# AV of two heads in two 64-column halves of the array, with the sums of weights in a matmul group of their own

## The chip, the cores and the metric

The kernel runs on one core of a Trainium2 chip. The metric is the device time of one execution in microseconds, as the median of several runs. A core has five engines with queues of their own: PE (matmuls; PEld are its weight loads), ACT (functions by table), DVE (elementwise work), POOL (elementwise work and the issue of some DMAs) and SP (issue of DMAs). PE reads two operands from SBUF: the weights, up to 128 columns that are loaded into the array, and the moving operand, whose columns stream through. It writes its result to PSUM, in banks of 128 partitions by 512 float32.

## The reference

Four batches, eight heads, a sequence of 768, 64 elements a head. Attention with a window of 96 positions, eight global keys and a bias by distance, then a gated FFN on the heads put side by side:

```python
scores = scale * q @ k.T + bias          # per head; bias falls with distance
scores = where(is_global | is_local, scores, -1e9)
a = softmax(scores)                      # exp, divided by the sum over keys
x = (a @ v), heads side by side          # 3072 tokens x 512
out = (relu(x @ w_gate) * (x @ w_val)) @ w_out   # 512 -> 1536 -> 512
```

## The kernel before

The work is cut into eight half-batches `s` of 384 queries. Each has an attention part, `attention_pieces(s)`, and an FFN part, `ffn_pieces(c)`, for the same tokens. The FFN of half-batch `c` is woven with the attention of `c + 1` by `weave`: after each FFN item, pieces of the attention are written out in proportion. No scheduler reorders it; each engine takes its instructions in the order of the code.

Heads are handled in four pairs `p`. Keys stand on partitions in tiles `j` of 120 local keys and the 8 global ones; there are 7 tiles for a batch, of which a first half-batch uses 4 and a second half-batch 5. For a pair, `piece_qk` (line 292) makes the scores of both heads in a qk_ps bank, transposed (keys on partitions, queries along the columns), ACT takes Exp into a tile `es` (line 306) and DVE multiplies by the factors of bias and mask `m_all` (line 315). For tile `j` a head has 3 x `w` query columns, 216 at most: 216, 216, 144 and 24 in a first half-batch, 72, 168, 192, 48 and 216 in a second one.

`piece_av(s, p, e)` (line 319) is called once for each head `e` of a pair. Its matmuls (line 331) have 128 columns of weights: 64 columns of V and 64 ones, so that a bank av_ps gets the head's output on 64 partitions and the sum of its weights, repeated, on the other 64. V lies in `vbuf` with a block of 64 ones between heads and at both ends; for head 0 of a pair the slice is [V | ones], for head 1 [ones | V], so the outputs of the pair fall on partitions 0 to 63 and 64 to 127. ACT takes Ln of the sums of each head (line 340, 64 partitions each, into one tile `lnd`), after head 1 Exp of minus that for both heads (line 345, the tile `rcp`), and then DVE multiplies each head's half bank by its part of `rcp` into `xT`, the FFN's moving operand (line 348). There are two av_ps banks; the next pair's first matmul needs a bank whose readers are through.

The FFN has 24 items of four matmuls (gate, line 375, and val, line 385) and 6 items of six matmuls (output, line 394). The gate of half-batch `c` needs all four pairs of `xT`.

Half-batches 0 and 1 are special. Their queries and keys are cast and transposed on PE (`piece_t`, line 250), with copies on DVE and ACT from one tp bank; later ones are transposed by DMA. The attention of half-batch 0 has no FFN beside it. The attention of half-batch 1 is woven into eight items of FFN 0; its queries and keys are loaded by SP behind two small memsets on DVE (line 159), which stand in the order of DVE behind a piece of pair 3 of half-batch 0. V is loaded by POOL's DMAs with a cast; the eight global rows are loaded into tile 0 and spread to the other tiles by a DMA of SP (line 125). The ones are filled by `fill` (line 150): four tiles of the first buffer by DVE at the start, ahead of and between the instructions that make `dd`, from which ACT makes `m_all`; three tiles and the seven of the second buffer by POOL.

Of the kernel before, what the change touches and what calls it, by code (L numbers as in the profile page):

```python
# [8 lines left out]
FP32 = mybir.dt.float32  # L9
BF16 = mybir.dt.bfloat16  # L10
AF = mybir.ActivationFunctionType
ALU = mybir.AluOpType
# [3 lines left out]
def kernel(  # L16
# [12 lines left out]
    nc = tc.nc  # L29

    B, H, S, D = q.shape
    NG = int(n_global)
    NL = int(n_local)
    DM = H * D
# [4 lines left out]
    QH = S // 2  # L39
    NN = 3  # L40
# [4 lines left out]
    NT = -(-S // KT)  # L45
    scale = 1.0 / math.sqrt(D)
# [7 lines left out]
    for half in range(2):  # L54
        for j in range(NT):
            w0 = PK * j - 128 * half
            a, b_ = max(0, w0), min(128, w0 + WQ)
# [6 lines left out]
    const = ctx.enter_context(tc.tile_pool(name="const", bufs=1))  # L64
# [4 lines left out]
    rc_pool = ctx.enter_context(tc.tile_pool(name="rc", bufs=2))  # L69
# [15 lines left out]
    vbuf = [const.tile([128, NT, (2 * H + 1) * D], BF16, name=f"vbuf{i}") for i in range(2)]  # L85
# [29 lines left out]
    def v_dst(b, r0, r1, j):  # L115
        t = vbuf[b % 2][r0:r1, j, D:]
        return t.rearrange("p (h z) -> p h z", z=2 * D)[:, :, 0:D]
# [5 lines left out]
    def spread_v_globals(b, j0=1, j1=NT):  # L123
        t = vbuf[b % 2]
        nc.sync.dma_start(
            out=t[0:NG, j0:j1, :],
            in_=t[0:NG, 0:1, :].to_broadcast([NG, j1 - j0, (2 * H + 1) * D]))
# [22 lines left out]
    def fill(eng, i, j):  # L150
        eng.memset(vbuf[i][:, j, :].bitcast(mybir.dt.uint32), 0x3F803F80)

# [16 lines left out]
    fill(nc.vector, 0, 0)  # L169
# [31 lines left out]
    fill(nc.vector, 0, 1)  # L201
    nc.vector.tensor_scalar(dd[0:NG, 1], ga, BIG, float(NL), op0=ALU.mult, op1=ALU.max)
    nc.vector.tensor_scalar(dd[0:NG, 0], gd, BIG, float(NL), op0=ALU.mult, op1=ALU.max)
    fill(nc.vector, 0, 2)
    fill(nc.vector, 0, 3)
# [10 lines left out]
    xT_of = {}  # L216
    es_of = {}
    av_of = {}
# [100 lines left out]
    def piece_av(s, p, e):  # L319
        b, half = divmod(s, 2)  # L320
        h = 2 * p + e
        vb = vbuf[b % 2]
        av = av_psum.tile([128, 512], FP32, name="av_ps")
        av_of[s, p, e] = av
        av3 = av[:, 0:QH].rearrange("d (n p) -> d n p", n=NN)
        todo = [t for bank in banks_of_half[half] for t in bank]
        for i, (j, a, w, m) in enumerate(todo):
            es, c = es_of[s, p, j]
            c += e * NN * w
            z0 = 2 * D * h + (D if e == 0 else 0)  # L330
            nc.tensor.matmul(av3[:, :, a : a + w],  # L331
                             lhsT=vb[:, j, z0 : z0 + 128],
                             rhs=es[:, c : c + NN * w].rearrange("k (n p) -> k n p", n=NN),
                             start=(i == 0), stop=(i == len(todo) - 1),
                             skip_group_check=True)
        o0, d0 = (0, 64) if e == 0 else (64, 0)
        if e == 0:
            av_of[s, p, "l"] = rc_pool.tile([128, QH], FP32, name="lnd")
        ln = av_of[s, p, "l"]
        nc.scalar.activation(ln[o0 : o0 + 64], av[d0 : d0 + 64, 0:QH], AF.Ln, bias=0.0, scale=1.0)  # L340
        if e == 1:
            if s not in xT_of:
                xT_of[s] = xt_pool.tile([128, N_DC, QH], BF16, name="xT")
            rc = rc_pool.tile([128, QH], FP32, name="rcp")
            nc.scalar.activation(rc, ln, AF.Exp, bias=0.0, scale=-1.0)  # L345
            for e_ in range(2):
                r = slice(64 * e_, 64 * e_ + 64)
                nc.vector.tensor_tensor(xT_of[s][r, p, :], av_of[s, p, e_][r, 0:QH], rc[r],  # L348
                                        op=ALU.mult)
# [96 lines left out]
    for j in range(4, NT):  # L446
        fill(nc.gpsimd, 0, j)
# [17 lines left out]
    for j in range(NT):  # L465
        fill(nc.gpsimd, 1, j)
# [60 lines left out]
```

## Time and profile before

| | |
|---|---|
| median of 3 runs | 295.73 us (295.42 to 295.73) |
| profiled execution | 296.74 us |
| its span on the core | 295.0 us |
| PE busy | 247.5 us, 84% |
| ACT busy | 162.9 us, 55% |
| DVE busy | 142.3 us, 48% |
| POOL busy | 97.7 us, 33% |

The span is the time from the first to the last instruction on the engines; some 1.7 us of the execution lie around it. Matmuls are pipelined: a record lasts from a matmul's start to the modelled end of its results, so records overlap, and what a matmul takes from the next one is read from start to start. In the time lines below, neighbours of one kind are merged, with their count behind an x, the idle time ahead of them in brackets and what ended it.

### The profile page before, as it was taken

What the parts mean: (1) busy time and instruction counts of PE and PEld (TensorE: products, weight loads), DVE (VectorE), ACT (ScalarE), POOL (GpSimd) and SP (SyncE); (2) the same over time, 40 slices, a digit from 0 to 9 for tenths busy, and PEclk for the clock granted to TensorE, in tenths of its full rate; (3) what the DMA queues carried; (4) which work ended last, traced back from release to release, by engine and by line L of the source; (5) the groups of instructions that cost most, each with busy time, mean ns of one, the idle gap of its engine ahead of it and who ended that gap; (6) DMA issues with size and microseconds to landing.
All of it is one profiled execution on the core that took longest, in us unless ns stands there. A gap on an engine that the chain in (4) does not pass through costs nothing.

```text
span 295.0 us, 4547 instructions
## 1 busy us (share of the span) xinstructions
PE 247.5 (84%) x1536; PEld 142.5 (48%) x1536; DVE 142.3 (48%) x362; ACT 162.9 (55%) x333; POOL 97.7 (33%) x240
## 2 busy tenths in 40 slices
PE   1355887549998974799999989999999899979994
PEld 0133354324564532466456645664566456645651
DVE  7556256662435430376347625762476155623420
ACT  8456327462335852376477647764776567644321
POOL 8990139800419000770604153051514300000000
PEclk9999999766999998699999999999999999999999
DMA  7999970928950018998395639638784510001002
GB/s 180 190 204 193 226 199 1 95 15 240 248 115 37 36 67 180 266 87 161 40 144 184 107 90 181 188 60 138 122 205 81 116 73 0 2 36 71 1 8 101
DMA packets 81199, 34.57 MB, mean 117 GB/s; under 512 B 56920, under 2 KB 77912, under 8 KB 81176
## 3 DMA queue, kind: packets, MB, share of 16 engines
q1 hardware_dynamic: 49320, 26.38, 35.3%
q0 software_dynamic: 31856, 7.91, 26.9%
q8 instruction: 12, 0.20, 0.3%
q14 instruction: 11, 0.09, 0.1%
HBM read 28.38 MB, written 6.29 MB: 118 GB/s over the span
## 4 chain that ended last, share of the span: by engine, by line
PE 69%; ACT 14%; DVE 10%; issue 2%; SPq 2%; DMA 1%; POOL 0%; ACTq 0%; DVEq 0%; POOLq 0%
PE ff_ps L385 20%; PE ff_ps L375 20%; PE ff_ps L394 17%; PE av_ps L331 6%; PE qk_ps L303 6%; ACT lnd L340 4%; DVE xT L348 4%; ACT rcp L345 3%; ACT es L306 3%; DVE es L315 2%; ACT osb L399 1%; SPq L276 1%; ACT m_all L213 1%; DVE ht L387 1%; DMA kN<-kc 1%
## 5 line engine op out<-in xcount | busy, mean ns | idle before, releaser
L375 PE MATMUL ff_ps<-xT,wg 128*128 128x384 bf16 x384 | 82.8, 339 | 2.9 <-DVE xT L348 2.7
L385 PE MATMUL ff_ps<-xT,wv 128*128 128x384 bf16 x384 | 82.2, 339 | 0.2
L387 DVE TENSOR_TENSOR ht<-ff_ps,grelu 128x384 bf16<-128x384 f32 x96 | 53.2, 555 | 42.9 <-PE ff_ps L385 41.4
L378 ACT ACTIVATE grelu<-ff_ps 128x384 bf16<-128x384 f32 x96 | 46.9, 489 | 45.5 <-PE ff_ps L375 21.9
L394 PE MATMUL ff_ps<-wo_sb,ht 128*128 128x512 bf16 x288 | 67.6, 378 | 0.0
L348 DVE TENSOR_TENSOR xT<-av_ps,rcp 64x384 bf16<-64x384 f32 x64 | 35.5, 555 | 59.3 <-ACT rcp L345 57.2
L306 ACT ACTIVATE es<-qk_ps 128x432 bf16<-128x432 f32 (+2 forms) x96 | 49.3, 529 | 20.5 <-PE qk_ps L303 18.4
L315 DVE TENSOR_TENSOR es<-es,m_all 128x432 bf16<-128x432 bf16 (+6 forms) x144 | 43.1, 331 | 32.3 <-ACT es L306 31.3
L303 PE MATMUL qk_ps<-qT,kT 128*128 128x432 bf16 (+6 forms) x144 | 34.8, 309 | 21.9 <-ACT es L306 8.7
L385 PEld LDWEIGHTS <-wv 128*128 128x128 bf16 x384 | 38.1, 101 | 30.4 <-issue 9.3
L375 PEld LDWEIGHTS <-wg 128*128 128x128 bf16 x384 | 37.7, 101 | 25.5 <-issue 4.9
L340 ACT ACTIVATE lnd<-av_ps 64x384 f32<-64x384 f32 x64 | 31.0, 485 | 23.2 <-PE av_ps L331 21.8
L331 PE MATMUL av_ps<-es,vbuf 128*128 128x216 bf16 (+5 forms) x288 | 30.7, 242 | 11.3 <-DVE xT L348 11.2
L394 PEld LDWEIGHTS <-ht 128*128 128x128 bf16 x288 | 26.8, 97 | 27.2
L331 PEld LDWEIGHTS <-vbuf 128*128 128x128 bf16 x288 | 25.3, 105 | 28.0 <-issue 19.1
L270 POOL CAST qz<-qs 128x192 bf16<-128x192 f32 x48 | 16.6, 372 | 41.2 <-issue 17.5
L399 ACT COPY osb<-ff_ps 128x512 f32<-128x512 f32 x24 | 14.0, 585 | 26.2 <-PE ff_ps L394 26.2
L303 PEld LDWEIGHTS <-kT 128*128 128x128 bf16 x144 | 14.2, 102 | 28.8 <-issue 11.5
L131 POOL DMA_DIRECT2D vbuf<-in_v_dram x28 | 24.3, 876 | 0.0
L246 POOL COPY kT<-kN 128x240 bf16<-128x240 bf16 x12 | 5.0, 416 | 41.7 <-DMA kN<-kc 41.7
L345 ACT ACTIVATE rcp<-lnd 128x384 f32<-128x384 f32 x32 | 16.7, 523 | 1.0
L242 POOL COPY kT<-kN 128x360 bf16<-128x360 bf16 x12 | 6.4, 536 | 29.0 <-DMA kN<-kc 29.0
(57 smaller groups left out, 88.9 us busy)
## 6 DMA issues: line engine op xcount, KB each, us to landing
out_dram<-osb SPq DMA_DIRECT2D x24, 256.0 KB, 2.0
qs<-in_q_dram SPq DMA_DIRECT2D x6, 768.0 KB, 7.1
ks<-in_k_dram SPq DMA_DIRECT2D x6, 768.0 KB, 10.1
vbuf<-in_v_dram POOLq DMA_DIRECT2D x24, 120.0 KB, 5.0
qs<-in_q_dram SPq DMA_DIRECT2D x8, 192.0 KB, 12.5
ks<-in_k_dram SPq DMA_DIRECT2D x8, 192.0 KB, 5.1
wg<-in_moe_w_gate_dram POOLq DMA_DIRECT2D x3, 512.0 KB, 7.4
wv<-in_moe_w_val_dram POOLq DMA_DIRECT2D x3, 512.0 KB, 9.2
```

Source lines behind the costliest of these rows:

```text
L303: nc.tensor.matmul(ps[:, c : c + n_], lhsT=kt[:, j, :], rhs=qd[:, :, :, a : a + w], start=True, stop=True)
L306: nc.scalar.activation(es[:, 0:cols], ps[:, 0:cols], AF.Exp, bias=0.0, scale=scale)
L315: nc.vector.tensor_mul(e4, e4, mk)
L331: nc.tensor.matmul(av3[:, :, a : a + w], lhsT=vb[:, j, z0 : z0 + 128], rhs=es[:, c : c + NN * w].rearrange("k (n p) -> k n p", n=NN), star ...
L340: nc.scalar.activation(ln[o0 : o0 + 64], av[d0 : d0 + 64, 0:QH], AF.Ln, bias=0.0, scale=1.0)
L345: nc.scalar.activation(rc, ln, AF.Exp, bias=0.0, scale=-1.0)
L348: nc.vector.tensor_tensor(xT_of[s][r, p, :], av_of[s, p, e_][r, 0:QH], rc[r], op=ALU.mult)
L375: nc.tensor.matmul(psg[:, 0:QH], lhsT=w_of(wg, dc, fc), rhs=xT[:, dc, :], start=(dc == 0), stop=(dc == N_DC - 1))
L378: nc.scalar.activation(gr, psg[:, 0:QH], AF.Relu, bias=0.0, scale=1.0)
L385: nc.tensor.matmul(psv[:, 0:QH], lhsT=w_of(wv, dc, fc), rhs=xT[:, dc, :], start=(dc == 0), stop=(dc == N_DC - 1))
L387: nc.vector.tensor_tensor(ht[:, fc, :], psv[:, 0:QH], st["gr"], op=ALU.mult)
L394: nc.tensor.matmul(ps2, lhsT=ht[:, fc, n * 128 : (n + 1) * 128], rhs=wo_sb[:, fc, :], start=(fc == 0), stop=(fc == N_FC - 1))
```

## The change

`vbuf` now holds V alone, 512 columns a tile. A tile `ones` of 128 x 64 is set once. `piece_av(s, p, what)` is still called twice for each pair, but by kind: with `what` 0 it makes the sums of both heads, with `ones` as weights, and with `what` 1 the outputs of both heads, with V as weights. In each, every key tile has two matmuls of 64 weight columns, head 0 into partitions 0 to 63 and head 1 into partitions 64 to 127 of the same bank; the program gives them array tiles of 128 rows by 64 columns, at columns 0 and 64. After the sums ACT takes Ln and Exp on 128 partitions; after V one multiplication on 128 partitions gives `xT`. The places of the two calls in the order are those of the two heads before. The fills go; the last tile of each V buffer, whose lower part no load covers, is set to zero once.

```diff
-    vbuf = [const.tile([128, NT, (2 * H + 1) * D], BF16, name=f"vbuf{i}") for i in range(2)]
+    vbuf = [const.tile([128, NT, DM], BF16, name=f"vbuf{i}") for i in range(2)]
+    ones = const.tile([128, D], BF16)
...
     def v_dst(b, r0, r1, j):
-        t = vbuf[b % 2][r0:r1, j, D:]
-        return t.rearrange("p (h z) -> p h z", z=2 * D)[:, :, 0:D]
+        return vbuf[b % 2][r0:r1, j, :].rearrange("p (h d) -> p h d", d=D)
...
-            in_=t[0:NG, 0:1, :].to_broadcast([NG, j1 - j0, (2 * H + 1) * D]))
+            in_=t[0:NG, 0:1, :].to_broadcast([NG, j1 - j0, DM]))
...
-    def fill(eng, i, j):
-        eng.memset(vbuf[i][:, j, :].bitcast(mybir.dt.uint32), 0x3F803F80)
...
-    fill(nc.vector, 0, 0)
+    nc.vector.memset(ones, 1.0)
+    nc.vector.memset(vbuf[0][:, NT - 1, :], 0.0)
...
-    fill(nc.vector, 0, 1)
     nc.vector.tensor_scalar(dd[0:NG, 1], ga, BIG, float(NL), op0=ALU.mult, op1=ALU.max)
     nc.vector.tensor_scalar(dd[0:NG, 0], gd, BIG, float(NL), op0=ALU.mult, op1=ALU.max)
-    fill(nc.vector, 0, 2)
-    fill(nc.vector, 0, 3)
...
-    def piece_av(s, p, e):
+    def piece_av(s, p, what):
+
         b, half = divmod(s, 2)
-        h = 2 * p + e
-        vb = vbuf[b % 2]
         av = av_psum.tile([128, 512], FP32, name="av_ps")
-        av_of[s, p, e] = av
         av3 = av[:, 0:QH].rearrange("d (n p) -> d n p", n=NN)
         todo = [t for bank in banks_of_half[half] for t in bank]
         for i, (j, a, w, m) in enumerate(todo):
             es, c = es_of[s, p, j]
-            c += e * NN * w
-            z0 = 2 * D * h + (D if e == 0 else 0)
-            nc.tensor.matmul(av3[:, :, a : a + w],
-                             lhsT=vb[:, j, z0 : z0 + 128],
-                             rhs=es[:, c : c + NN * w].rearrange("k (n p) -> k n p", n=NN),
-                             start=(i == 0), stop=(i == len(todo) - 1),
-                             skip_group_check=True)
-        o0, d0 = (0, 64) if e == 0 else (64, 0)
-        if e == 0:
-            av_of[s, p, "l"] = rc_pool.tile([128, QH], FP32, name="lnd")
-        ln = av_of[s, p, "l"]
-        nc.scalar.activation(ln[o0 : o0 + 64], av[d0 : d0 + 64, 0:QH], AF.Ln, bias=0.0, scale=1.0)
-        if e == 1:
+            for e in range(2):
+                h = 2 * p + e
+                ce = c + e * NN * w
+                nc.tensor.matmul(av3[64 * e : 64 * e + 64, :, a : a + w],
+                                 lhsT=ones if what == 0 else vbuf[b % 2][:, j, D * h : D * h + D],
+                                 rhs=es[:, ce : ce + NN * w].rearrange("k (n p) -> k n p", n=NN),
+                                 start=(i == 0), stop=(i == len(todo) - 1),
+                                 skip_group_check=True)
+        if what == 0:
+            ln = rc_pool.tile([128, QH], FP32, name="lnd")
+            nc.scalar.activation(ln, av[:, 0:QH], AF.Ln, bias=0.0, scale=1.0)
+            rc = rc_pool.tile([128, QH], FP32, name="rcp")
+            nc.scalar.activation(rc, ln, AF.Exp, bias=0.0, scale=-1.0)
+            av_of[s, p] = rc
+        else:
             if s not in xT_of:
                 xT_of[s] = xt_pool.tile([128, N_DC, QH], BF16, name="xT")
-            rc = rc_pool.tile([128, QH], FP32, name="rcp")
-            nc.scalar.activation(rc, ln, AF.Exp, bias=0.0, scale=-1.0)
-            for e_ in range(2):
-                r = slice(64 * e_, 64 * e_ + 64)
-                nc.vector.tensor_tensor(xT_of[s][r, p, :], av_of[s, p, e_][r, 0:QH], rc[r],
-                                        op=ALU.mult)
+            nc.vector.tensor_tensor(xT_of[s][:, p, :], av[:, 0:QH], av_of[s, p], op=ALU.mult)
...
-    for j in range(4, NT):
-        fill(nc.gpsimd, 0, j)
...
-    for j in range(NT):
-        fill(nc.gpsimd, 1, j)
+    nc.gpsimd.memset(vbuf[1][:, NT - 1, :].bitcast(mybir.dt.uint32), 0)
```

PE's order at the seam between the two pieces of pair 0 of half-batch 0; es0 to es2 are the pair's score tiles, the number behind av_ps tells one bank's use from another's. Before, the last key tile of head 0 and then head 1:

```order
L331 LDWEIGHTS vbuf0_101
L331 MATMUL av_ps_297<-es2_223,vbuf0_101 128x3x8
L331 LDWEIGHTS vbuf0_101
L331 MATMUL av_ps_304<-es0_213,vbuf0_101 128x3x72
L331 LDWEIGHTS vbuf0_101
L331 MATMUL av_ps_304<-es1_218,vbuf0_101 128x3x72
```

And now the end of the sums and the beginning of V:

```order
L325 LDWEIGHTS ones_103
L325 MATMUL av_ps_296<-es2_222,ones_103 64x3x8
L325 LDWEIGHTS vbuf0_101
L325 MATMUL av_ps_309<-es0_212,vbuf0_101 64x3x72
L325 LDWEIGHTS vbuf0_101
L325 MATMUL av_ps_309<-es0_212,vbuf0_101 64x3x72
L325 LDWEIGHTS vbuf0_101
L325 MATMUL av_ps_309<-es1_217,vbuf0_101 64x3x72
```

Each tile of `es` now has two matmuls in a row, one for each head, on 64 partitions, and each bank holds both heads.

DVE's order in half-batch 0, from the last mask of pair 2's scores over the copies of pair 3's queries and keys (qT, kT) to the first mask of pair 3's. Before:

```order
L315 TENSOR_TENSOR es_291<-es_291,m_all 128x48
L348 TENSOR_TENSOR xT<-av_ps,rcp 64x384 x2
L262 COPY qT_111<-tp 64x384
L263 COPY qT_111<-tp 64x384
L243 COPY kT_3_106<-tp 128x24
L244 COPY kT_3_106<-kT_3_106 128x7x8
L348 TENSOR_TENSOR xT<-av_ps,rcp 64x384 x2
L315 TENSOR_TENSOR es_345<-es_345,m_all 128x432
```

And now:

```order
L310 TENSOR_TENSOR es_290<-es_290,m_all 128x48
L339 TENSOR_TENSOR xT<-av_ps,rcp 128x384
L257 COPY qT_112<-tp 64x384
L258 COPY qT_112<-tp 64x384
L238 COPY kT_3_107<-tp 128x24
L239 COPY kT_3_107<-kT_3_107 128x7x8
L339 TENSOR_TENSOR xT<-av_ps,rcp 128x384
L310 TENSOR_TENSOR es_356<-es_356,m_all 128x432
```

One multiplication into xT stands where two stood, ahead of the copies and ahead of the masks; nothing else changes place.

## Rows read from the trace of the kernel before

**Rows 1.** The page, part 1: busy us, share of the span, instructions.

```profile
PE 247.5 (84%) x1536; PEld 142.5 (48%) x1536; DVE 142.3 (48%) x362; ACT 162.9 (55%) x333; POOL 97.7 (33%) x240
```

**Rows 2.** Waits of PE: who for whom, us in total, times, longest.

```profile
PE av_ps L331 <- DVE xT L348: 11.2, 10, 1.9
...
PE ff_ps L375 <- DVE xT L348: 2.7, 2, 1.3
```

**Rows 3.** Groups by line and shape: count, busy us, mean ns, idle before.

```profile
L348 DVE TENSOR_TENSOR xT<-av_ps,rcp 64x384 bf16<-64x384 f32 x64 | 35.5, 555 | 59.3 <-ACT rcp L345 57.2 <-PE ff_ps L375 1.2
L340 ACT ACTIVATE lnd<-av_ps 64x384 f32<-64x384 f32 x64 | 31.0, 485 | 23.2 <-PE av_ps L331 21.8
...
L331 PEld LDWEIGHTS <-vbuf 128*128 128x128 bf16 x288 | 25.3, 105 | 28.0 <-issue 19.1 <-DVE xT L348 0.3
...
L345 ACT ACTIVATE rcp<-lnd 128x384 f32<-128x384 f32 x32 | 16.7, 523 | 1.0
```

**Rows 4.** Time line of PE, half-batch 4: start us, us, what, count.

```profile
155.45 0.81 PE L375 MATMUL ff_ps<-xT,wg 128*128 128x384 bf16 x4
156.10 0.42 PE L331 MATMUL av_ps<-es,vbuf 128*128 128x216 bf16 x4
156.38 0.81 PE L385 MATMUL ff_ps<-xT,wv 128*128 128x384 bf16 x4
...
175.13 0.42 PE L331 MATMUL av_ps<-es,vbuf 128*128 128x216 bf16 x4 [0.75 <-DVE xT L348]
```

**Rows 5.** Time line of PE, half-batch 7.

```profile
253.92 0.47 PE L331 MATMUL av_ps<-es,vbuf 128*128 128x72 bf16 x5
254.23 0.81 PE L385 MATMUL ff_ps<-xT,wv 128*128 128x384 bf16 x4
```

**Rows 6.** Time line of PE and DVE, half-batch 0.

```profile
19.18 1.18 PE L331 MATMUL av_ps<-es,vbuf 128*128 128x216 bf16 x8
...
20.21 0.80 PE L257 MATMUL tp<-ident,qk 128*128 128x128 bf16 x6
...
22.08 1.28 PE L331 MATMUL av_ps<-es,vbuf 128*128 128x216 bf16 x8 [1.07 <-DVE xT L348]
...
24.47 0.88 PE L303 MATMUL qk_ps<-qT,kT 128*128 128x432 bf16 x2 [1.11 <-ACT lnd L340]
...
27.32 0.06 DVE L159 MEMSET qs<- 1x4 f32 x1
...
29.12 1.28 PE L331 MATMUL av_ps<-es,vbuf 128*128 128x216 bf16 x8 [1.71 <-DVE xT L348]
...
32.70 0.48 PE L375 MATMUL ff_ps<-xT,wg 128*128 128x384 bf16 x1 [1.34 <-DVE xT L348]
```

**Rows 7.** Time line of POOL and PE, half-batch 1.

```profile
40.74 0.51 POOL L227 CAST qk<-ks 128x384 bf16<-128x384 f32 x1 [2.38 <-DMA ks<-in_k_dram]
...
42.83 0.49 PE L257 MATMUL tp<-ident,qk 128*128 128x128 bf16 x6 [1.11 <-DVE kT L248]
...
55.00 0.52 PE L303 MATMUL qk_ps<-qT,kT 128*128 128x432 bf16 x1 [3.16 <-ACT es L306]
```

**Rows 8.** Time line of DVE and ACT, the start.

```profile
1.21 0.51 DVE L151 MEMSET vbuf<- 128x544 uint32 x1
...
3.62 0.51 DVE L151 MEMSET vbuf<- 128x544 uint32 x1
...
4.53 3.73 ACT L213 ACTIVATE m_all<-dd 128x432 bf16<-128x432 f32 x8 [0.43 <-DVE dd L203]
```

**Rows 9.** One stretch: length, busy PE, PEld, DVE, ACT, POOL, PEclk, DMA, GB/s.

```profile
42.80:66.40 23.60, 14.06 (x106) 9.35 (x107) 14.59 (x46) 13.77 (x30) 14.70 (x28) 0.83 0.55 36
```

**Rows 10.** The chain in order of time, after it: start us, us, what.

```profile
66.79 1.28 PE ff_ps L385 x4
...
72.65 0.65 PE ff_ps L375 x4
```

## The prediction

> **What bounds the kernel now.** I read the busy times first, then who waits for whom on PE, then the time line of PE in the even stretch, and then of all engines in the two half-batches that stand ahead of it. PE is the busiest engine, 247.5 us of the span of 295.0, DVE and ACT are at about half [rows 1]. So an operation saved on ACT or DVE counts where PE waits for it, and a matmul column added counts nearly everywhere. The waits of PE [rows 2] say where the first can be: the AV matmuls wait for DVE's multiplication into xT ten times, 11.2 us in all, and the gate matmuls wait for the last xT of a half-batch twice, 2.7 us. The reason is in the buffers: a pair of heads takes both av_ps banks, and neither is given back before Ln, Ln, Exp and two multiplications are through. By their durations [rows 3] that is 2 x 485 + 523 + 2 x 555 = 2.6 us, less what overlaps. In the even stretch PE does two 1.3 us FFN items meanwhile and waits 0.75 us only where AV pieces of two pairs stand close together [rows 4].
>
> The even stretch, from half-batch 2 on, has PE back to back. An AV piece of a first half-batch starts at 156.10 and the next group at 156.38 [rows 4]: 0.28 us for 600 columns (216, 216, 144 and 24). A piece of a second half takes 253.92 to 254.23, 0.31 us, for 696 columns [rows 5]. Both are what the columns take one after another at the full clock, with weight loads hidden although each is recorded with 105 ns [rows 3]. That is the number on which this prediction turns.
>
> **The change, part by part. ACT and DVE.** Ln runs once a pair on 128 partitions instead of twice on 64, the multiplication into xT too. The time goes by the 384 columns, so each pair saves 485 ns on ACT and 555 ns on DVE [rows 3], 15.5 and 17.8 us over 32 pairs. On the even stretch this is hidden under PE. What counts is what the order gives: sums come first, so Ln and Exp run while V's matmuls run; the sums' bank is free after one Ln, V's after one multiplication. Then (a) the 11.2 us of AV waits go; (b) the last pair of half-batches 0 and 1 has after its last matmul one multiplication (0.56) instead of Ln, Exp and two multiplications, and the gate's first three matmuls cover that: the 2.7 us go; (c) two QK waits of 1.11 us at 24.47 [rows 6] and 3.16 us at 55.00 [rows 7] have one multiplication and one Ln less queued ahead of their copies on DVE and ACT, 1.04 us each, 2.1 us.
>
> **Start.** Two of the four fills of V's ones on DVE, 0.51 us each, stand ahead of dd, for which the masks of m_all wait [rows 8]. They become two smaller memsets. ACT itself is busy with copies to within 0.43 us of m_all's start, so (d) at most 0.4 us. The ten fills on POOL, the shorter V rows in the spread, and V's memset hide beside DMA that POOL's next casts wait for; I take nothing for them.
>
> Sum of (a) to (d): 11.2 + 2.7 + 2.1 + 0.4 = 16.4 us.
>
> **What is late next.** Half-batch 1's keys: POOL's cast at 40.74 waited for the DMA and ends at 41.25, and PE's transposes that need it started at 42.83 [rows 7]. So of what half-batch 0 gains before them, 1.07 + 1.71 + 1.34 + 1.04 + 0.4 = 5.6 us [rows 6], only 1.6 us fit if the loads land when they did. The loads are issued behind a memset on DVE at 27.32 [rows 6] that itself moves up by about 1.9 us (one Ln and one multiplication of pair 0, the start, and the Ln of pair 1 that no longer precedes the Exp of pair 3's scores). If they land that much sooner, 3.5 us fit. I take 2.6 us.
>
> The granted clock is 0.83 over half-batch 1's stretch, with PE idle for 40% of it, and after it four FFN groups take 1.28 us each where they later take 0.65 [rows 9, 10]: 2.5 us at the half level. With fewer gaps they may run at the full one, or the fall may come at another place; I take 0 and leave 2.5 us either way in the ranges.
>
> **PE.** Before, one matmul of 128 weight columns gives V and sums of one head. After, each of the two pieces of a pair has a matmul for each head, 64 columns of weights in its half of the array: twice the matmuls (576 for 288) with the same moving columns each. The trace shows no matmul in less than the whole array, so the cost is bounded. Below: the two halves stream side by side, a piece stays at 0.28 or 0.31 us, extra 0. Above: they take turns, as every two matmuls in this trace do, and a piece doubles: 24 x 0.28 + 24 x 0.31 = 14.2 us in half-batches 2 to 7. In half-batch 0 a piece takes (20.21 - 19.18) / 2 = 0.51 us [rows 6] and is on the path only where Ln or the multiplication is waited for, about four of its eight: 2.1 us; in half-batch 1 likewise half of eight at 0.4, 1.6 us. With turns half-batch 0 then gains 5.6 - 2.1 = 3.5 and gives back only 0.9. Weight loads: two of half the size where one was, hidden as the 105 ns are now; 0, with the bound in the first rival.
>
> I take the turns, since these are the only rows there are on two matmuls. Sum: -16.4 + 0.9 + 14.2 + 2.1 + 1.6 = +2.4 us. The profiled execution took 296.74 us (span 295.0 and 1.7 around it), so 299.1 there; its time is 1.0 above the median of the runs, 295.73, so **298.1 us** as a median.
>
> **Rivals. First, the halves overlap.** Then PE pays nothing and half-batch 0 gives back 5.6 - 2.6 = 3.0 us: -16.4 + 3.0 = -13.4, 282.3 us. For it: the two matmuls use other columns of the array, other moving data and other PSUM partitions. Against it: no row shows two matmuls at a time. If loads of 64 weights show, at half of 105 ns each, a pair of halves can't go faster than 0.105 us against 0.092 for 216 columns; eight loads then take 0.42 us for 0.28 and ten 0.52 for 0.31, on 48 pieces +8.4 us: 290.7. The Trainium skill, "TensorEngine Tiling (Array Packing)", Key Properties, says that tiles operate independently and can load and multiply in parallel; by that rule this rival is the case. No row here can show it.
>
> **Second, the array empties at each change between whole and half.** A change stands wherever AV work meets FFN or QK work: 100 runs' ends in the new order, 86 of them from half-batch 2 on. Price: four gate matmuls are recorded with 0.81 us and the next group starts 0.65 us after them [rows 4], so 0.16 us of a group's end lies under the next group today. If the next must wait for that, 86 x 0.16 = 13.8 us. With turns 298.1 + 13.8 = 311.9, with overlap 282.3 + 13.8 = 296.1. The same page and section says that changing the tiling mode, not just the tile, drains TensorE; by that rule this rival holds on top of either. The rows can't tell.
>
> **Third, the waits come back in another place:** V's piece of the next pair needs V's bank, which waits for Exp and its multiplication. Where two pairs stand side by side (ends of half-batches 0, 1, 2 and 7), and where ACT's queue holds other work ahead of Ln, half of the 11.2 and all of the 2.1 could stay: with turns 298.1 + 7.7 = 305.8. Against it: ACT is at 55% [rows 1], and in the even stretch an FFN item stands between.
>
> The first rival ends faster, the others and the forecast slower; what decides is the extra time of a piece on PE. Per piece 0.29 us is the turns, 0 is overlap; the two cancel the gain of 13 to 15 us where a piece costs about 0.25 us more on some 56 pieces.
>
> **How the numbers follow.** Turns 0.40, its own range 292 to 304 (gains of 16.4 less a quarter to a half, or all of the keys' slack). Overlap 0.36. Emptying 0.17, two thirds of it with turns. Waits elsewhere 0.07. About 0.2% (0.6 us) is what a measurement can tell from no change. Faster: 0.35 of the overlap and 0.09 of the turns' lower end, 0.44; same: 0.03 of the turns, 0.03 of overlap with emptying, 0.06; slower 0.50. The range runs from the overlap to emptying with turns, 282 to 312.
>
> **What would show it.** The starts of AV matmuls: in an even stretch a piece of eight takes 0.55 us with turns, 0.28 with overlap; a pair of halves starting within a few ns says overlap. The gap from the last FFN matmul's start to the first AV matmul, and back: 0.16 for FFN as now, about 0.32 if the array empties. PE's wait for xT at L331's successor: near 0 of 11.2. First gate matmul stalled on xT in half-batch 0 by less than 0.3 us; half-batch 1's transposes waiting for POOL's cast. Wrong it would be if pieces get dearer than twice, or if the gains of half-batches 0 and 1 end in the DMA wait entirely.

## The result

The changed kernel takes 285.2 us (median of 4 runs, 284.1 to 285.9) where the kernel before takes 295.6: a ratio of 0.965, 95% interval 0.961 to 0.968. Here and below, medians and ratios leave out the few runs in which a kernel was in the chip's slower state. The profiled execution has a span of 283.5 us, 11.4 less than before. The range of the prediction held it; its forecast, 298.1 and slower, had the wrong sign. The first rival, halves that overlap, was the case, with about half of the second's price on top of it.

**The profile after.** The busy line of the page, and under it the shares of the chain that ended last; compare with [rows 1]:

```profile
PE 250.5 (88%) x1824; PEld 138.6 (49%) x1824; DVE 123.0 (43%) x328; ACT 147.7 (52%) x301; POOL 93.7 (33%) x231
...
PE 77%; ACT 7%; DMA 6%; DVE 4%; SPq 3%; issue 1%; POOL 0%; ACTq 0%; DVEq 0%; POOLq 0%
```

PE has 288 more matmuls and 3 us more busy time, in a shorter span. ACT and DVE lost 15 and 19 us of busy time, for 15.5 and 17.8 worked out (DVE lost its fills too). Who waits for whom on PE, first rows of that view (us in total, times, longest), to be set against [rows 2], and the two groups that answer to [rows 3]:

```profile
PE qk_ps L298 <- DVE kT L239: 8.2, 3, 3.5
PE qk_ps L298 <- ACT es L301: 6.2, 10, 1.6
PE tp L252 <- DVE qk L222: 4.3, 1, 4.3
PE qk_ps L298 <- DMA qT<-qz: 4.1, 1, 4.1
PE av_ps L325 <- ACT lnd L332: 1.7, 4, 0.6
```

```profile
L339 DVE TENSOR_TENSOR xT<-av_ps,rcp 128x384 bf16<-128x384 f32 x32 | 17.8, 555 | 37.2 <-PE av_ps L325 29.9 <-ACT rcp L334 5.7 <-ACT grelu L368 1.1
...
L332 ACT ACTIVATE lnd<-av_ps 128x384 f32<-128x384 f32 x32 | 15.8, 494 | 17.4 <-PE av_ps L325 17.4
...
L325 PEld LDWEIGHTS <-vbuf 128*64 128x64 bf16 x288 | 11.6, 114 | 10.1 <-issue 10.1
```

Of the 11.2 us that AV waited for xT, 0.4 are left, and 1.7 us have come in which it waits for one Ln; the gate's waits for xT are gone. An operation on 128 partitions takes what one on 64 took (555 ns for 555, and 494 for 485), so half of the time is saved.

The time line of PE in half-batch 4, the place of [rows 4] (start us, us, what, count):

```profile
142.39 0.81 PE L365 MATMUL ff_ps<-xT,wg 128*128 128x384 bf16 x4
143.13 0.45 PE L325 MATMUL av_ps<-es,ones 128*64 128x216 bf16 x8
143.51 0.82 PE L375 MATMUL ff_ps<-xT,wv 128*128 128x384 bf16 x4
```

A visit to the AV matmuls takes 143.51 - 143.13 = 0.38 us for 0.28 before, and the FFN group ahead of it 143.13 - 142.39 = 0.74 for 0.65. Eight matmuls with 1200 moving columns in all fit in 0.38 us: the halves run at the same time. About 0.09 us is lost on entering and 0.08 to 0.10 on leaving. The raw starts in the trace say the same: the two halves of a pair start 3 to 4 ns apart, and the next pair 0.12, 0.09 and 0.06 us later, the distances at which single matmuls of 216, 216 and 144 columns stood before, with 0.03 more at the first.

The time line of PE over the ends of half-batches 0 and 1, the places of [rows 6 and 7]:

```profile
23.31 0.52 PE L298 MATMUL qk_ps<-qT,kT 128*128 128x432 bf16 x2 [1.01 <-ACT lnd L332]
...
26.84 0.71 PE L325 MATMUL av_ps<-es,vbuf 128*64 128x216 bf16 x8 [0.58 <-ACT lnd L332]
27.49 1.46 PE L365 MATMUL ff_ps<-xT,wg 128*128 128x384 bf16 x4
...
38.48 0.34 PE L252 MATMUL tp<-ident,qk 128*128 128x128 bf16 x3 [0.24 <-POOL qk L222]
...
49.64 0.34 PE L298 MATMUL qk_ps<-qT,kT 128*128 128x432 bf16 x1 [1.58 <-ACT es L301]
...
55.45 1.11 PE L365 MATMUL ff_ps<-xT,wg 128*128 128x384 bf16 x4
56.40 0.81 PE L375 MATMUL ff_ps<-xT,wv 128*128 128x384 bf16 x4
57.05 0.81 PE L365 MATMUL ff_ps<-xT,wg 128*128 128x384 bf16 x4
```

The four gate matmuls from 27.49 wait for nothing; before, the fourth of them waited 1.34 us [rows 6]. And after half-batch 1 the second FFN group takes 57.05 - 56.40 = 0.65 us, the full granted clock, where four groups took 1.28 [rows 10]. The stretch that answers to [rows 9], same columns:

```profile
38.20:62.20 24.00, 18.37 (x180) 11.16 (x180) 14.33 (x46) 14.10 (x31) 12.99 (x26) 1.00 0.93 142
```

PE was busy for 77% of it, not 60%, and the granted clock stayed 1.00 (the 2.4 GHz level) for 0.83.

**Where the time went**, by the start of the same matmul in both traces (after minus before): -4.3 us at the fourth gate matmul of FFN 0, -4.9 at the first transposes of half-batch 1, -8.4 at its end (the gate matmul at 55.45), -12.8 eight gate items later (66.15 us in the changed kernel), -14.1 at the first gate matmul of FFN 2 (99.32), and from there on 2.7 us are lost again: -11.4 at the end. So the gain is all made in the first 100 us, and the even stretch is a small loss. The 4.5 us that are gained between the matmuls at 55.45 and 66.15 are for the greater part the granted clock: before, it was at its half level from 61.7 to 72.0 us, in the changed kernel at the full level from 32.2 to 103.9 us.

### The profile page after: what moved, and what is told of

It reads as the page before. It is cut to its first block, busy times and chain, and to the rows that moved or that the text cites. A ratio compares the mean times of both kernels' runs of the same rounds, so it can differ in the third digit from the quotient of the medians.

```text
span 283.5 us, 5047 instructions
## 1 busy us (share of the span) xinstructions
PE 250.5 (88%) x1824; PEld 138.6 (49%) x1824; DVE 123.0 (43%) x328; ACT 147.7 (52%) x301; POOL 93.7 (33%) x231
## 4 chain that ended last, share of the span: by engine, by line
PE 77%; ACT 7%; DMA 6%; DVE 4%; SPq 3%; issue 1%; POOL 0%; ACTq 0%; DVEq 0%; POOLq 0%
PE ff_ps L375 21%; PE ff_ps L384 21%; PE ff_ps L365 21%; PE av_ps L325 8%; PE qk_ps L298 6%; DMA ks<-in_k_dram 5%; ACT es L301 2%; SPq L271 1%; ACT m_all L208 1%; DVE es L310 1%; SPq L274 1%; DMA kN<-kc 1%; SPq L111 1%; DVE qT L258 1%; ACT lnd L332 1%
## 5 line engine op out<-in xcount | busy, mean ns | idle before, releaser
L375 PE MATMUL ff_ps<-xT,wv 128*128 128x384 bf16 x384 | 80.7, 334 | 0.0
L365 PE MATMUL ff_ps<-xT,wg 128*128 128x384 bf16 x384 | 80.4, 332 | 0.1
L298 PE MATMUL qk_ps<-qT,kT 128*128 128x432 bf16 (+6 forms) x144 | 33.9, 304 | 20.7 <-DVE kT L239 8.2
L375 PEld LDWEIGHTS <-wv 128*128 128x128 bf16 x384 | 37.1, 100 | 26.6 <-issue 3.9
L365 PEld LDWEIGHTS <-wg 128*128 128x128 bf16 x384 | 36.3, 99 | 24.6 <-issue 1.8
L339 DVE TENSOR_TENSOR xT<-av_ps,rcp 128x384 bf16<-128x384 f32 x32 | 17.8, 555 | 37.2 <-PE av_ps L325 29.9
L389 ACT COPY osb<-ff_ps 128x512 f32<-128x512 f32 x24 | 14.1, 586 | 30.2 <-PE ff_ps L384 30.2
L332 ACT ACTIVATE lnd<-av_ps 128x384 f32<-128x384 f32 x32 | 15.8, 494 | 17.4 <-PE av_ps L325 17.4
L325 PEld LDWEIGHTS <-ones 128*64 128x64 bf16 x288 | 11.4, 113 | 13.4 <-issue 12.7
L325 PE MATMUL av_ps<-es,vbuf 128*64 128x216 bf16 (+6 forms) x288 | 15.7, 237 | 1.6 <-ACT lnd L332 1.2
L325 PEld LDWEIGHTS <-vbuf 128*64 128x64 bf16 x288 | 11.6, 114 | 10.1 <-issue 10.1
## 6 DMA issues: line engine op xcount, KB each, us to landing
qs<-in_q_dram SPq DMA_DIRECT2D x8, 192.0 KB, 12.8
```

Source lines behind the costliest of these rows:

```text
L298: nc.tensor.matmul(ps[:, c : c + n_], lhsT=kt[:, j, :], rhs=qd[:, :, :, a : a + w], start=True, stop=True)
L325: nc.tensor.matmul(av3[64 * e : 64 * e + 64, :, a : a + w], lhsT=ones if what == 0 else vbuf[b % 2][:, j, D * h : D * h + D], rhs=es[:, ce ...
L332: nc.scalar.activation(ln, av[:, 0:QH], AF.Ln, bias=0.0, scale=1.0)
L339: nc.vector.tensor_tensor(xT_of[s][:, p, :], av[:, 0:QH], av_of[s, p], op=ALU.mult)
L365: nc.tensor.matmul(psg[:, 0:QH], lhsT=w_of(wg, dc, fc), rhs=xT[:, dc, :], start=(dc == 0), stop=(dc == N_DC - 1))
L375: nc.tensor.matmul(psv[:, 0:QH], lhsT=w_of(wv, dc, fc), rhs=xT[:, dc, :], start=(dc == 0), stop=(dc == N_DC - 1))
```

## The experiments

The theories. **Overlap**: the two halves run at once, a change between whole and half array costs about 0.19 us a visit (a visit is one run of AV matmuls between other work), and what is gained at the front is gained by saved operations and the new order. **Turns**, the forecast: halves follow one another, and the gain comes from elsewhere. Each edit is against the changed kernel, and the diffs show its main lines. The runs were made on several chips, and the changed kernel itself was not run again beside them. The kernel before was, with medians of 295.3 to 296.0 us, so a difference from the changed kernel's 285.2 of under a microsecond says nothing.

### The order of the halves

```diff
-        for i, (j, a, w, m) in enumerate(todo):
-            es, c = es_of[s, p, j]
-            for e in range(2):
-                h = 2 * p + e
+        for e in range(2):
+            h = 2 * p + e
+            for i, (j, a, w, m) in enumerate(todo):
+                es, c = es_of[s, p, j]
```

> The changed kernel with the two loops of piece_av swapped: all key tiles of head 0 in the left half of the array, then all of head 1 in the right half, so that two matmuls in a row use the same half. Same matmuls, same columns, same order of everything else. If the halves streaming side by side carries the gain, a piece takes twice its 0.28 or 0.31 us: 48 pieces from half-batch 2 on cost 14.2 us more and the first two some 3, 285.2 + 14 to 17 = 299 to 302 us, slower than the kernel before. If the gain is the new order and the fewer operations on ACT and DVE alone, nothing changes: 285 us. If weights of 64 columns in the same half can't be loaded under the running matmul, it is dearer still, over 303.

Measured: 287.4 us, ratio to before 0.970 (0.966 to 0.975). PE's time line, half-batch 4:

```profile
143.64 0.81 PE L365 MATMUL ff_ps<-xT,wg 128*128 128x384 bf16 x4
144.38 0.46 PE L325 MATMUL av_ps<-es,ones 128*64 128x216 bf16 x8
144.77 0.82 PE L375 MATMUL ff_ps<-xT,wv 128*128 128x384 bf16 x4
```

The edit did not make turns: the visit takes 0.39 us again. By the trace's records the matmuls start in pairs of equal size (216, 216; 216, 216; 144, 144; 24, 24), 13 ns apart, although the program issues all of head 0 ahead of all of head 1; in a second half-batch, with five sizes, head 1's follow head 0's by 0.06 us. So the edit put none of the expectations to the test; it took another way to get turns, the two that follow.

### Turns on the whole array

V between blocks of zeros, ones between blocks of zeros, so that each head has a matmul of 128 weight columns that adds zeros to the other's half; order and operations of the changed kernel, but the layout and fills of before.

```diff
-                nc.tensor.matmul(av3[64 * e : 64 * e + 64, :, a : a + w],
-                                 lhsT=ones if what == 0 else vbuf[b % 2][:, j, D * h : D * h + D],
+                z0 = 2 * D * h + (D if e == 0 else 0)
+                nc.tensor.matmul(av3[:, :, a : a + w],
+                                 lhsT=ones[:, D * e : D * e + 128] if what == 0 else vbuf[b % 2][:, j, z0 : z0 + 128],
```

> The new order, one Ln and one multiplication a pair, but no halves: V lies between blocks of zeros, the ones likewise, and each head's matmul has 128 columns of weights, [V | 0] or [0 | V], that add into the same bank. Twice the matmuls of the kernel before, each on the whole array, no change between whole and half. This is the turns of the prediction: its sum says 298.1. By the changed kernel's trace: 285.2 + 14.2 + about 3 in the first half-batches - 43 visits x 0.18 us = 294 to 295. If changes between whole and half cost nothing, 302.

Measured: 293.0 us, ratio 0.989 (0.986 to 0.992). PE's time line, half-batch 4:

```profile
148.31 0.69 PE L334 MATMUL av_ps<-es,vbuf 128*128 128x216 bf16 x8
148.86 0.81 PE L374 MATMUL ff_ps<-xT,wg 128*128 128x384 bf16 x4
149.51 0.35 PE L306 MATMUL qk_ps<-qT,kT 128*128 128x432 bf16 x1
```

Here are the turns as they were priced: 0.55 us a piece (148.86 - 148.31), and no gap ahead of the next group. This is the case that the forecast of 298.1 describes, only that it still has the old layout and fills, which the forecast had gone. So at least 5 us of my error lie outside the question of turns: even with turns the kernel is faster than before.

### Turns within one half

The two calls made by head again, sums and V of head 0 in the left half of two banks, then both of head 1 in the right half. Both banks are held until the end of the pair, as before the change.

```diff
-            for e in range(2):
-                h = 2 * p + e
...
+        for what in range(2):
+            av3 = av_of[s, p][what][:, 0:QH].rearrange("d (n p) -> d n p", n=NN)
```

> Visits by head instead of by kind: one visit has the sums and the V products of head 0, all in the left half, the next those of head 1, all in the right half; Ln, Exp and one multiplication after the second. Same matmuls in halves, but a visit never has work for both halves. If each half takes its matmuls in turn and the two only run side by side when both have work, a visit takes 0.55 or 0.62 us and its two changes 0.18: 14.2 us more from half-batch 2 on, and both banks are held until the end as in the kernel before, so some waits for xT return: 299 to 306 us. If 64-column matmuls are cheap for another reason than the side by side, 286 to 290.

Measured: 303.3 us, ratio 1.026 (1.020 to 1.032): slower than before.

```profile
150.74 0.45 PE L326 MATMUL av_ps<-es,ones 128*64 128x216 bf16 x4
151.04 0.43 PE L326 MATMUL av_ps<-es,vbuf 128*64 128x216 bf16 x4
151.40 0.82 PE L374 MATMUL ff_ps<-xT,wv 128*128 128x384 bf16 x4
```

A visit takes 0.66 us for 0.38 with as many matmuls of the same sizes and the same changes: within one half they do take turns. In the stretch from the first gate matmul of FFN 2 to that of FFN 7, with 39 visits, the starts of successive matmuls, summed from the trace's records in us, show what each form pays (the rest of a stretch is between matmuls of FFN and scores):

| | stretch | inside AV | from FFN into AV | from AV into FFN |
|---|---|---|---|---|
| before | 154.2 | 11.1 (1.7 of it waits) | 10.9 (2.9 of it waits) | 2.6 |
| whole array, turns | 158.6 | 20.9 | 7.4 | 2.9 |
| one half, turns | 170.0 | 23.4 | 11.0 | 6.1 |
| changed kernel | 156.9 | 10.3 | 11.0 | 6.1 |

Overlap gives 10.6 us against turns on the whole array; the changes cost 3.6 + 3.2 = 6.8, 0.17 us a visit. Net this is 3.8 us, and the stretch is 1.7 shorter; most of the rest is the granted clock, at its half level for 3.4 us of the stretch on the whole array and for 6.8 in the changed kernel. Against before, a visit that waits for nothing costs about 0.2 us more: 0.09 on entering, 0.08 to 0.10 on leaving and 0.03 inside. So next to turns on the whole array, halves gain little in all: the kernel with halves and all fills, below, which has the same layout, takes 290.4 us for 293.0, and the intervals of the two ratios overlap.

### Fewer visits

From half-batch 2 on both pieces of a pair in one visit, so that the kernel has 31 visits in all for 50.

```diff
+        if s >= 2:
+            AV = lambda p: [(0.28, lambda: (piece_av(s, p, 0), piece_av(s, p, 1))), (0.28, lambda: None)]
```

> The changed kernel with both pieces of a pair, sums and V, written out together from half-batch 2 on, at the place of the sums: 31 visits to the halves instead of 50. If a visit costs the 0.18 us that the gaps at its two ends show, 19 x 0.18 = 3.4 us less: 281.8. If the gaps are hidden by slack elsewhere, 285. If V's piece then waits for its bank or the scores, or ACT and DVE come in bursts, more than 285.

Measured: 282.0 us, ratio 0.953 (0.947 to 0.959): faster than both kernels.

```profile
143.41 0.81 PE L367 MATMUL ff_ps<-xT,wg 128*128 128x384 bf16 x4
144.15 0.45 PE L325 MATMUL av_ps<-es,ones 128*64 128x216 bf16 x8
144.45 0.43 PE L325 MATMUL av_ps<-es,vbuf 128*64 128x216 bf16 x8
144.81 0.82 PE L377 MATMUL ff_ps<-xT,wv 128*128 128x384 bf16 x4
```

A visit with both pieces takes 0.66 us, 2 x 0.28 and one change out. By the medians 3.3 us are saved with 19 visits, 0.17 each. In the traces the stretch of the table, which holds all 19, is 2.1 us shorter although it has a new wait of 1.9 us (the gate matmul at 116.57, for DVE's product): 0.21 each. Both fit the price as a cost of the visit, not of the piece.

### The saved operations

Ln and the multiplication as two operations of 64 partitions each, then each alone. The edit for Ln:

```diff
-            nc.scalar.activation(ln, av[:, 0:QH], AF.Ln, bias=0.0, scale=1.0)
+            for e in range(2):
+                r = slice(64 * e, 64 * e + 64)
+                nc.scalar.activation(ln[r], av[r, 0:QH], AF.Ln, bias=0.0, scale=1.0)
```

> The changed kernel with the operations of ACT and DVE as many as before: Ln in two of 64 partitions, the multiplication into xT in two of 64 partitions; array and order as changed. If the saved operations matter (15.5 us of ACT, 17.8 us of DVE in all), several us come back, 290 or more. If what counts is that the sums' bank comes free early and that Ln and Exp run beside V's matmuls, only the tails of half-batches 0 to 2 and the copies behind them get 0.5 to 1 us longer each: 287 to 288.

> The changed kernel with Ln alone in two operations of 64 partitions; one multiplication. Splitting both cost 9 us. If the chain of half-batches 0 and 1 through ACT carries that, Ln alone (0.49 us more for each pair) brings back about half: 288 to 290 us. If it is the multiplication on DVE ahead of the copies for the next pair, Ln alone costs 1 us or less: 286.

> The changed kernel with the multiplication into xT alone as two of 64 partitions, 555 ns more of DVE a pair. Both operations split (e3_split_ops) cost 8.9 us, Ln alone (e7_ln_split) 5.6. If the two add up, 288 to 289, most of it before the first gate matmuls of half-batch 0 (28.43 in the changed kernel) and at the clock of half-batch 1. If DVE's operation is hidden unless ACT's is split too, 285 to 286; if each of them alone costs nearly the whole, 290 or more.

Measured: both split 294.1 us (0.995, 0.991 to 0.999), Ln alone 290.1 (0.983, 0.977 to 0.989), the multiplication alone 289.3 (0.980, 0.975 to 0.986). Against the changed kernel that is 8.9, 4.8 and 4.1 us by the medians, 9.5, 4.8 and 2.7 by the profiled spans. PE's time line with both split, end of half-batch 0:

```profile
28.27 0.71 PE L325 MATMUL av_ps<-es,ones 128*64 128x216 bf16 x8 [0.55 <-ACT lnd L334]
30.05 0.71 PE L325 MATMUL av_ps<-es,vbuf 128*64 128x216 bf16 x8 [1.07 <-ACT lnd L334]
...
32.05 0.48 PE L369 MATMUL ff_ps<-xT,wg 128*128 128x384 bf16 x1 [0.21 <-DVE xT L343]
```

V's last piece starts at 30.05 for 26.84 in the changed kernel. By the starts of the same matmuls the two splits cost 3.6 us up to the fourth gate matmul of FFN 0, 5.3 at the end of half-batch 1, 7.8 at the matmul that the changed kernel has at 66.15 (the half level of the clock comes back at 59.3 to 66.1 us), 9.1 at the first gate matmul of FFN 2, and 0.4 after that. So nearly the whole gain needs the saved operations, in the half-batches where ACT, DVE and PE wait for each other in a chain. All the rest of the change without them (order, overlap, layout) is worth 0.5% of the time, about 1.5 us (0.4 to 2.6). The gain isn't theirs alone: the next section takes 5.2 us away by another part, and the parts don't add up to 10.4.

### The layout of V and the fills

Overlap, order and operations of the changed kernel, but V with its gaps, all fills and the wide spread as before.

```diff
-    vbuf = [const.tile([128, NT, DM], BF16, name=f"vbuf{i}") for i in range(2)]
+    vbuf = [const.tile([128, NT, (2 * H + 1) * D], BF16, name=f"vbuf{i}") for i in range(2)]
```

> The changed kernel with the old V buffers: a block of ones between heads, the four fills on DVE at the start and the ten on POOL, V's slices of 64 columns taken from between them, the wider rows in the spread. Matmuls and operations as changed. By the trace of the changed kernel the start's gain (scores of pair 0 at 8.61 for 9.18 us) is gone by pair 2 (17.80 for 17.78), so nothing comes back: 285 to 286 us. If the fills on DVE or POOL were on the path, or the narrower buffer made the DMAs faster, 286.5 or more.

Measured: 290.4 us, ratio 0.984 (0.977 to 0.991), 5.2 us over the changed kernel. Its profiled run is the fastest of the four (288.9 to 291.8): the span is 287.2, 3.6 over the changed kernel's, and only these can be read from the trace. Time line of DVE and POOL at the keys of pair 1:

```profile
13.41 1.91 DVE L246 COPY kT<-kT 128x56 bf16<-128x56 bf16 x1
13.47 1.56 POOL L152 MEMSET vbuf<- 128x544 uint32 x3
13.49 2.03 DVE L229 CAST qk<-qs 128x384 bf16<-128x384 f32 x1
```

A copy that takes 0.17 us in both other kernels ends 0.3 us after POOL's three fills, and pair 1's scores start 1.8 us late; 2.3 us of delay are there at the end of half-batch 1. The same fills met the same two instructions in the kernel before, and there POOL's took longer instead (1.78 us for 1.56):

```profile
13.34 0.17 DVE L244 COPY kT<-kT 128x56 bf16<-128x56 bf16 x1
13.41 1.78 POOL L151 MEMSET vbuf<- 128x544 uint32 x3
13.42 0.79 DVE L227 CAST qk<-qs 128x384 bf16<-128x384 f32 x1
```

Three more runs take this apart: POOL's three fills alone, DVE's four alone (both into a tile that nobody reads), and this kernel with one of POOL's three.

```diff
+    for j in range(4, NT):
+        fill(nc.gpsimd, j)
```

> The changed kernel with POOL's first three fills put back at their place, into a tile that nobody reads, so that they only take POOL's time and nothing waits for them. Kept old layout and all fills (e4_fills) cost 5 us against the changed kernel. If POOL's fills are what holds DVE's copy of pair 1's keys up there (1.91 us where it takes 0.17), that copy is long here too, PE's scores of pair 1 (13.65 in the changed kernel) start some 1.8 us later, nothing is late at the first transposes (4.32), and the median is 287 to 288.5. If the copy was long for the wider V rows or for the other fills, it takes 0.17 here, pair 1 starts within 0.1 us of the changed kernel's, and the median is 285 to 286.

> The changed kernel with DVE's four fills of 0.51 us put back at their places at the start, into a tile that nobody reads. If these are what e4_fills pays for, the first transposes come 1.8 us after the changed kernel's 4.32, and as the rest of half-batch 0 is a chain of latencies this stays: 286.5 to 287.5. If the start has slack behind it (my term d, 0.4 us at most, since ACT's copies end close to the start of m_all), the first transposes are later but the scores of pair 1 are within 0.5 us of 13.65, and the median is 285 to 286.

> The kernel of e4_fills (old layout of V, all fills) with one of POOL's first three fills instead of three, at the same place; the two tiles that are no longer filled hold V where it is read and nothing is read between. There DVE's copy of pair 1's keys took 1.91 us, from 13.41 to the end of POOL's three fills. If POOL's memset holds DVE up, the copy now ends with the one fill: about 0.6 to 0.9 us, pair 1's scores some 1.0 us earlier than in e4_fills (15.47), and the median 1 to 3 us under its 290.4. If the copy waited for something else, it keeps its 1.9 us and the median stays at 289 to 291.

Measured: POOL's alone 285.8 us (0.966, 0.963 to 0.970), DVE's alone 285.9 (0.966, 0.964 to 0.969), one of POOL's three 290.1 (0.981, 0.972 to 0.990). The same time line with POOL's fills alone, and then with one of the three:

```profile
12.57 0.27 DVE L243 COPY kT<-kT 128x56 bf16<-128x56 bf16 x1
...
13.56 1.56 POOL L152 MEMSET spare<- 128x544 uint32 x3
```

```profile
13.41 0.17 DVE L246 COPY kT<-kT 128x56 bf16<-128x56 bf16 x1
13.47 0.59 POOL L152 MEMSET vbuf<- 128x544 uint32 x1
13.49 0.78 DVE L229 CAST qk<-qs 128x384 bf16<-128x384 f32 x1
```

So neither group of fills costs anything measurable alone: DVE's make the first transposes 2.1 us late, of which 0.35 are left at pair 1's scores, and POOL's fell a microsecond behind DVE's copy. What the kernel with all fills paid at the front is a meeting of two instructions at one moment, and the kernel before shows that such a meeting need not cost DVE anything. What decides it stays open. With one fill the copy is short, shorter than the first expectation had it (0.17 us for 0.6 to 0.9), and from pair 1's scores to 66 us PE's starts are within 0.3 us of the changed kernel's. But the median, 290.1 us for 290.4, isn't lower by the 1 to 3 us of that expectation. Its profiled run, 293.5 us, was the slowest of the four (the others 287.3 to 291.0), so of its trace only the front is read, and what kept its time up stays open.

With all fills a second cost stands at half-batch 2. SP's queue, the spread of V's global rows and the keys of half-batch 2, in the changed kernel, then with all fills; under the latter PE's first scores of half-batch 2:

```profile
57.33 1.44 SPq L125 DMA_DIRECT2D vbuf<-vbuf  x1
...
59.36 1.83 SPq L111 DMA_DIRECT2D ks<-in_k_dram  x1
```

```profile
59.66 2.19 SPq L126 DMA_DIRECT2D vbuf<-vbuf  x1
...
62.43 1.90 SPq L111 DMA_DIRECT2D ks<-in_k_dram  x1
...
81.55 0.54 PE L305 MATMUL qk_ps<-qT,kT 128*128 128x432 bf16 x2 [1.21 <-POOL kT L246]
```

PE runs 2.3 us behind the changed kernel here, and SP's loads start as much later. The spread then takes 0.75 us longer, the keys are issued 3.1 us later, and POOL's first cast of them starts 4.7 us later (68.18 for 63.46). The fills of the second buffer stand ahead of V's loads on POOL (seven take 3.50 us, the one memset 0.32), and the last of these loads is issued 3.3 us later (its issue ends at 57.65 for 54.36); that these loads, or the wider rows of the spread, are what holds the keys is argued from the order, not shown. It costs 1.2 us, where the changed kernel has no such wait. In the kernel before PE comes to these scores at 90.69 us and doesn't wait either.

### The tail of half-batches 0 and 1

On top of the joined visits, the last two pairs as sums, sums, V, V.

```diff
+        TAIL = [(0.28, lambda p=p, e=e: piece_av(s, p, e)) for e in range(2) for p in (2, 3)]
```

> The joined visits (281.97 us) and, in half-batches 0 and 1, the last two pairs in the order sums 2, sums 3, V 2, V 3, so that V of pair 3 waits for Ln of pair 3 and not for the multiplication of pair 2. The waits of V 3 in the changed kernel are 0.6 us and more in each: 1 to 2 us less than the joined visits, 280 to 281. If Exp of pair 3 ends last anyway, no change: 282.

Measured: 281.8 us, ratio 0.954 (0.948 to 0.959): no difference from the joined visits alone (282.0). The fourth gate matmul of FFN 0 came only 0.3 us sooner. PE's time line in half-batch 1:

```profile
35.10 0.34 PE L252 MATMUL tp<-ident,qk 128*128 128x128 bf16 x3 [1.25 <-POOL qk L222]
...
39.15 0.50 PE L252 MATMUL tp<-ident,qk 128*128 128x128 bf16 x3 [1.62 <-POOL qk L222]
```

The transposes now wait for POOL's cast, that is for the load of the keys: the limit that I had named for the gain of half-batch 0 is reached about here. The granted clock differs as well: it was at its half level from 24.7 to 28.2 and again from 38.4 to 45.2 us, with the joined visits alone from 25.5 to 32.3.

## Why the prediction was wrong

**"I take the turns, since these are the only rows there are on two matmuls" is the step that failed.** No row of the trace before showed two matmuls at a time, because none was in less than the whole array; that was no evidence for turns. I had 0.36 for overlap beside 0.40 for turns, and took the larger. A pair of halves starts within 4 ns, a piece inside itself costs what it did but for 0.03 us, and the 17.9 us of turns in the sum were 0. The kernel that does take turns measured 293.0, with the old layout: its sign, too, was not the forecast's, so the turns alone don't account for the miss.

**The change of mode** was a rival of its own and holds in kind: the Trainium skill, "TensorEngine Tiling (Array Packing)", Key Properties, has both the independence of tiles and the drain at a change of mode, and this trace agrees with both: pairs 3 to 4 ns apart, and a loss of 0.09 us in and 0.08 to 0.10 out. The price was mis-sized: 86 x 0.16 = 13.8 us were forecast; 43 visits from half-batch 2 on at 0.17 are 7.3 us. Had I taken overlap with this price, the sum would have been 282.3 + 7.3 = 289.6.

**Between that and 285.2 lie 4.4 us, and between 298.1 and the 293.0 of turns 5.1: the terms of the front gave too little.** By their parts, which overlap and need not add up to the 4.4:

- (a) 11.2 and (b) 2.7 us of waits for xT: gone but for 0.4, with 1.7 us of waits for Ln in their place. Right.
- (c) 2.1 us for two QK waits: the one of 3.16 is 1.58 now, the one of 1.11 is still 1.01. 1.7 us, about right as a term; but of the gain I put only this down to saved operations, while splitting them again costs 8.9 us. Most of (a) and (b) in half-batches 0 and 1 needs them and doesn't come of the order alone, as I had it.
- (d) 0.4 us at the start: 0.35 with DVE's fills put back. Right.
- POOL's fills and the shorter V rows, taken at nothing because DMA was to hide them: with them and DVE's fills back in the changed kernel it takes 5.2 us more, of which the trace shows 2.3 at the front and 1.2 at half-batch 2's keys. What they cost the kernel before no run shows.
- The give-back of 0.9, or 3.0 with overlap, did not come. The loads were issued 2.3 us sooner (25.12 for 27.42), near the 1.9 I had; but the keys whose cast started at 40.74 [rows 7] were cast at 37.92, 2.8 sooner, and with the 1.6 us of slack the whole gain of half-batch 0, 4.3 us for the 5.6 that I had, fitted. I had taken 2.6 where my own numbers, 1.9 and the slack, gave 3.5. In the overlap case this term was 3.0 us too dear, and half-batch 0 gained 1.3 less than I had: 1.7 us of the error.
- The clock, taken as 0 with 2.5 us either way: the four groups of [rows 10] ran at the full level. From the end of half-batch 1 to the matmul at 66.15 the changed kernel gained 4.5 us, 1.4 of them the gate's second wait [rows 2] and about 3.1 the clock, 0.6 over my bound. I had the rows that priced it in hand. With PE busy for 77% of half-batch 1's stretch instead of 60% the clock was at the full level there; what made it stay there no run isolates.

The signs that the prediction named did their work: by the time of a piece, 0.55 us with turns and 0.28 with overlap, and by a pair of halves starting within a few ns, the trace tells the two apart.

## What to carry to other kernels

Two matmuls of 64 weight columns, set in the two halves of the array, cost the time of one; what is paid is the way in and out, 0.17 us a visit here, so gather them in few visits. Saving an operation on an engine that is half idle is worth next to nothing in a stretch where PE is back to back (0.4 us after the first 100 us here), and much of its length where engines wait for each other in a chain: of the 4.2 us that the two splits add over four pairs, 3.6 counted in half-batch 0 and 1.7 in half-batch 1. The granted clock, at the half level behind half-batch 1 in the kernel with both split, added 2.5. Where a trace can't show a mechanism, its absence there is no evidence for the other one.

## What the runs showed of the hardware

**Halves take their work past each other.** With all of head 0 issued ahead of all of head 1, matmuls of the two halves still started in pairs, 13 ns apart in half-batch 4, where alternating order has 3 to 4, and 39 visits cost 1.4 us more inside than with alternating order. That the engine was given the matmuls in the program's order is taken from the program; the trace shows only their starts.

**A copy on DVE was held up beside POOL's memsets, in one trace.** A copy of 0.17 us took 1.91 beside three fills of POOL and ended 0.3 us after them. In another kernel, with the same two starts to the hundredth and one fill, the copy was short and the cast behind it took 0.78 us; in the kernel before, with three fills from 0.07 us after the copy's start, the copy was short, the cast took 0.79 (0.54 in the changed kernel, without fills) and the fills 1.78 for 1.56. The Trainium skill, "SBUF — State Buffer", Who interferes with whom, describes a port pair that some copies and casts of DVE share with POOL, and that whichever issues first holds for a whole instruction. A long copy in one trace and longer fills in another agree with that; that the later starter, POOL at 13.47, held up the copy recorded from 13.41 does not follow from the starts in the trace.
